# Linear attention and an MLP-Mixer block: the last 64 rows of all batches done as a ninth batch, and work moved from VectorE to ScalarE and GpSimd

## The chip, the cores and the metric

One core of a Trainium2 chip runs the whole program. The time is that of one execution on the device in microseconds; the median of several runs is given, and times are compared with those of the kernel before on the same chip. The engines have queues of their own and meet only through semaphores: TensorE (PE: matmul, with its weight loads, PEld), VectorE (DVE), ScalarE (ACT), GpSimd (POOL) and SyncE (SP, which here only issues transfers). The number behind an L is a line of the kernel before.

## What is computed

Eight batches, 8 heads, 576 positions, head dimension 64; the types are float32 at the outside.

```python
def _attn_ref(q, k, v):
    def phi(x):
        return np.where(x > 0, x, np.exp(x) - 1.0) + 1.0
    q_p, k_p = (phi(q), phi(k))
    kv = np.einsum('bhsd,bhse->bhde', k_p, v)
    z = np.sum(k_p, axis=2)
    num = np.einsum('bhsd,bhde->bhse', q_p, kv)
    den = np.einsum('bhsd,bhd->bhs', q_p, z)[..., None] + 1e-06
    return num / den

def _moe_ref(x, w_tok1, w_tok2, w_ch1, w_ch2):     # x: the heads side by side, 576 x 512 per batch
    xt = x.transpose(0, 2, 1)
    h = np.maximum(xt @ w_tok1, 0.0) @ w_tok2      # 576 -> 256 -> 576
    u = x + h.transpose(0, 2, 1)
    h2 = np.maximum(u @ w_ch1, 0.0) @ w_ch2        # 512 -> 1536 -> 512
    return u + h2
```

## The kernel before

**Tiling.** A batch's 576 positions are 64 partitions times 9; two of the nine share a tile of 128 rows, so a batch has four full tiles and a half one of 64 rows, its *tail*. Two batches' tails fill one tile: batches 2p and 2p+1 are pair p.

**An order written out by hand.** Every piece of work is a Python closure with a short name (`put`), and the string `ORDER` (L66) lists the names; each engine's queue holds its pieces in that order. No scheduler moves anything. `BANK` (L42) gives each result its PSUM bank, `SLOT` (L58) its place among the output slots of `obuf` (6 of 512 columns), `ON_DVE` (L36) the pieces that VectorE does where ScalarE would. A name begins with its batch: `3Lk0` loads half of k of batch 3 (on SP, float32, into one set of buffers that batches 0 and 2 to 7 share; batch 1 has its own), `3kx0` takes exp on ScalarE (L252), `3ka0` and `3kb0` finish phi on VectorE (L256, L262), `3v0` casts v (L275), `3K` is the kv product (L302), `3Kc0` its copy (L308), `3qT0` transposes q by a DMA on SP (L335).

**Numerators and denominators.** `3n` multiplies q by kv, 40 matmuls of 65 columns (64 numerators and their denominator) into three pairs of banks (L387). `3nd` and `3ne` take the reciprocals (L400, L402; L405, L407), then VectorE multiplies: three blocks of six heads-and-tiles, `3n0`, `3n1`, `3n2` (L413), and two single ones, `3o0`, `3o1` (L422). Batch 1 has a form of its own (`nd1_mm`, L352: 20 matmuls of 130 columns, in six groups with a reciprocal and a multiply each, L361 to L364).

**Token mixing.** `3f0`, `3f1` (L448), their relu on ScalarE (L452), `3g0`, `3g1` (L459), the add of x on VectorE (`3gu0`, L470), and the transposition of u by DMA (`3uT0`, L489). Batch 1 does the last steps by PE and copies (`1h`, L520 to L533; `1t`, `1tc`, L538 to L543). Tails: `3gt` makes those of a pair (L478), VectorE adds x into one of two tiles `ut` (L483), and a DMA transposes it (`3ut`, L494); pair 0 is transposed by PE (L672, L676).

**Channel mixing of the full tiles.** Batch 0, and batch 1's first layer, are plain matmuls (L686, L747). The rest treats each product as 2 x 2 blocks and takes it by seven block products, whose sums and differences of inputs are made beforehand. First layer: sums of u (`3s1` to `3s4`, VectorE, L885), of the weights once for all batches (`G`, into `swc`, L897), and for each of three groups seven products of four matmuls of 256 columns (`3x05` is product 5 of group 0, L928) with reads `3y05`: three copies and one relu by ScalarE (L943, L941), three add-and-relu by VectorE (L681). Batch 7 does not use `swc` but makes sums of its own (`7F`, GpSimd L869 and VectorE L836). Second layer: row sums of the activations (`3w`, L836), weight sums (`ws`, `wt`, once), seven products in two halves of six matmuls of 256 columns (`3p50`, L970). Three partial results are copied to SBUF by ScalarE (`3c0` to `3c2`, L1058); the four quarters of the output, Z, W, Y and X, are ended by VectorE, which adds u (`3eZ`, ..., L1064); GpSimd adds a copied part to Z, W and Y (`3hZ`, ..., L1071) and issues the stores (`3o`, L1075). Batches 1 to 6 use the same four output slots. Batch 7's ends are cut into 14 reads (`7R`, L984) and stores on SP and ScalarE's queue (`7D`, L990).

**Channel mixing of the tails.** Pairs 0 and 1, each in the middle of the order: `T00` to `T12` are 48 matmuls of 128 columns each pair (L711), read by ScalarE (L715), `U` 12 of 512 (L747), `V` the add of u (L760, output slots 4 and 5), `W` the stores by GpSimd. Pairs 2 and 3, at the end beside batch 7: `7c` is 48 matmuls of 256 columns (L733), read by ScalarE (L737), four sums by GpSimd (`7ts`, L836), seven products of six matmuls (`7t`, L1024), seven reads by VectorE (`7tr`, L1031), and stores of 128 KB.

Of the kernel before, what the change touches and what calls it, by code (L numbers as in the profile page):

```python
# [17 lines left out]
NO = 6  # L18
# [11 lines left out]
CUTS = {1: [0, 3, 6], 2: [0, 2, 6], 3: [0, 2, 6], 4: [0, 2, 6], 5: [0, 2, 6], 6: [0, 2, 6], 7: [0, 2, 4, 6]}  # L30
# [5 lines left out]
ON_DVE = {'1v0', '2v1', '0r3', '0r6', '0r9', '1r5', '1r8'}  # L36
# [3 lines left out]
WHOLE = {'00', '01', 't0', 't1'}  # L40

BANK = {k_: int(v_) for k_, v_ in (e.split(":") for e in """2K:0 2n0:0 2n1:2 2n2:4 2f:6 2g0:3 2g1:6 2X2:5 2Z2:2 2Y2:1 2gt:6 3K:6 3n0:2 3n1:4 3n2:6 3f:3 3g0:6 3g1:6 3X2:2  # L42
3Z2:0 3Y2:5 3gt:4 4K:2 4n0:2 4n1:4 4n2:6 4f:6 4g0:4 4g1:0 4X2:2 4Z2:1 4Y2:3 4gt:6 5K:6 5n0:1 5n1:3 5n2:5 5f:5
5g0:5 5g1:3 5X2:4 5Z2:5 5Y2:7 5gt:1 6K:2 6n0:1 6n1:3 6n2:5 6f:2 6g0:5 6g1:2 6X2:4 6Z2:0 6Y2:6 6gt:6 7K:2 7n0:2
7n1:4 7n2:6 7f:2 7g0:0 7g1:2 7X2:3 7Z2:6 7Y2:1 7gt:5 2m2:0 2m3:1 2m4:2 2m5:3 2m8:1 2m9:1 2m10:0 2m11:1 3m2:0
3m3:1 3m4:2 3m5:3 3m8:1 3m9:0 3m10:0 3m11:1 4m2:0 4m3:1 4m4:2 4m5:3 4m8:1 4m9:1 4m10:0 4m11:1 5m2:0 5m3:1
5m4:2 5m5:3 5m8:1 5m9:0 5m10:0 5m11:1 6m2:0 6m3:1 6m4:2 6m5:3 6m8:1 6m9:1 6m10:0 6m11:1 1h00:7 1h01:6 1h10:5
1h11:6 1t0:7 1t1:0 1t2:1 1t3:6 1m0:2 1m1:0 1m2:0 1m3:4 1m4:5 1m5:6 1m6:6 1m7:2 1m8:5 1m9:7 1m10:1 1m11:6 T00:7
T10:3 T01:3 T11:0 T02:3 T12:7 U08:0 U18:3 7c0:3 7c1:4 7c2:4 7c3:6 7c4:2 7c5:4 7X0:5 7Z0:4 7Y0:1 7X1:2 7Z1:0
7Y1:0 7PX0:7 7PZ0:3 7PY0:1 7PX1:6 7PZ1:5 7PY1:5 7tX:0 7tZ:4 7tY:2 1PX:1 1PZ:2 1PY:5 2PX:0 2PZ:5 2PY:1 3PX:0  # L50
3PZ:3 3PY:4 4PX:7 4PZ:0 4PY:0 5PX:0 5PZ:7 5PY:1 6PX:7 6PZ:1 6PY:6 warm0:0 0Q00:1 0Q01:2 0s0:3 warm1:0 0Q10:1
0Q11:2 warm2:3 0K0:4 0d0:0 0n0:6 0l0:1 0s1:2 0K1:4 0d1:3 0n1:6 0l1:0 0f0:1 0f1:4 0g00:2 0g01:3 0g10:0 0t0:6
0t1:4 0g11:1 0m0:3 0m1:7 0t2:6 0t3:4 0m2:1 0m3:2 0gt:2 0m4:5 0m5:6 0m6:6 0m7:3 0m8:7 0m9:0 0m10:4 0m11:4 U00:1
U01:0 1Q0:4 U02:2 U03:3 1Q1:6 1K:4 1n00:6 1n01:6 1n10:4 1n11:4 1n20:4 1n21:6 1f:4 1g2:4 0ut:3 2X1:6 2Z1:4
2Y1:2 3X1:3 3Z1:5 3Y1:1 4X1:7 4Z1:0 4Y1:0 5X1:6 5Z1:0 5Y1:2 6X1:5 6Z1:6 6Y1:1 2X0:7 2Z0:3 2Y0:0 3X0:4 3Z0:0
3Y0:6 4X0:1 4Z0:7 4Y0:5 5X0:1 5Z0:5 5Y0:0 6X0:7 6Z0:3 6Y0:2""".split())}

SLOT = {k_: int(v_) for k_, v_ in (e.split(":") for e in """0o0:0 0o1:2 1P:0 V0:4 2P:0 3P:0 V1:4 4P:0 5P:0 6P:0 7P0:4 7t:0 7P1:2""".split())}  # L58
# [7 lines left out]
ORDER = """A2 A0 A1 A3 A4 A5 A6 A8 A9 A7 A10 A12 A13 A14 A11 A16 A17 A15 A19 A18 A21 A20 A22 A23 A24 A25 A26 A27 A28 A29  # L66
A30 A33 A31 A32 A35 A34 A36 A37 A38 1Lk0 A39 1Lk1 1Lv1 A40 1Lq0 A41 1Lq1 A42 1Lv0 A43 0ma0 At2 0ma1 At3 0ma3
0mb1 0mb0 0ma6 0r0 0mb3 0r1 1ka0 0ma7 1kx0 0ma2 0ma8 0mb6 1kb0 0mb2 0r3 0mb8 0mb7 0r6 0r8 0ma4 0r7 G21 0gt
1kx1 G22 0ma9 0gv 0ma10 0mb4 1ka1 0r2 0ma5 0r4 G11 0mb10 1kb1 0mb5 0r10 G23 0mb9 0r5 0ma11 0mb11 1qa0 1qx0 B0
0r9 0q0 B1 0r11 1qb0 B2 1qx1 1qa1 1Q00 1Q01 0q1 1Qc01 1v0 1Qc00 0q2 1qb1 1v1 1Q10 1Q11 1K 1Qc11 2Lq0 ws02  # L70
1Qc10 0q3 2Lq1 1Kc0 1Kc1 2Lv0 ws04 1n20 1n01 2Lk0 1nc20 0q4 2Lk1 1nc01 2Lv1 1n10 0q5 1nc10 1n00 0q6 1nc00 1n11
0q7 1nc11 2qx0 1n21 ws14 0q8 1nc21 1f0 2qx1 2qa0 1f1 wt2 3Lq0 G24 0q9 1fr1 2qb0 1fr0 0q10 2qa1 2v0 G12 1h01
2qb1 1h00 1hu01 2qT1 ws00 0q11 1hu00 0z1 2kx0 1h10 2qT0 ws10 0z0 1h11 1hu10 1t0 1hu11 1t1 3Lv0 ws24 1g2 1tc1
1tc0 1t2 3Lq1 1t3 1gu2 1ma9 1tc3 ws12 0z2 1ma1 1ma5 1tc2 1ma4 0z3 1mb1 2v1 0o1 1mb5 1r1 1ma7 2ka0 2kx1 1mb7
G01 3Lk0 1ma10 0o0 G03 3qx0 1mb4 2kb0 0ut 1ma2 2ka1 1r4 1mb10 wt0 3Lk1 1mb2 1r7 1ma3 3Lv1 1r2 2kb1 1mb9 1r10
1ma8 3qa0 0uc 1mb8 1r5 ws20 1r9 2K 1r8 1mb3 2Kc0 2Kc1 3qb0 1ma6 1r3 2n ws30 2nd 1mb6 T00 2o0 ws34 1r6 2n1
1ma11 Tr00 2o1 ws22 1mb11 2ne 3v0 2n0 1ma0 1mb0 3qa1 T01 4Lv0 1r0 2n2 ws32 1r11 1p10 3qx1 2f0 1w13 G02 Tr01
# [38 lines left out]
def kernel(  # L116
# [1081 lines left out]
```

## Time and profile before

| | before |
|---|---|
| median of 3 runs (us) | 245.37 (245.18 to 245.67) |
| the profiled execution (us) | 245.24 |
| its span, first to last instruction (us) | 243.4 |
| granted TensorE clock | 0.998 |
| DVE busy between 72 and 80 us | 8.00 of 8.00 |
| ACT busy between 112 and 120 us | 7.16 of 8.00 |
| POOL busy between 112 and 120 us | 4.23 of 8.00 |
| loads of k, q and v (576 KB each), median from issue to landing (us) | 6.8, 6.3, 7.6 |
| stores by GpSimd, 512 KB, issue to landing (us) | 6.0 |
| DMA transposes of q, u and tails, issue to landing (us) | 4.7, 3.1, 2.5 |

"Busy" is the union of the instructions of an engine; matmuls overlap, so PE's busy time is not a measure of work done, and the spacing of matmuls must be read beside it. The line of an operation is that of the closure in which it stands. The groups of the costliest operations that the change touches (line, engine, operation, out <- in, shape, count | busy us, mean ns of one | idle before):

```profile
L711 PE MATMUL ps<-uTt,wc 128*128 128x128 bf16 x96 | 6.3, 219 | 0.1
L733 PE MATMUL ps<-uTt,wc 128*128 128x256 bf16 x48 | 5.9, 273 | 0.0
L413 DVE TENSOR_TENSOR x<-ps,dens 128x768 bf16<-128x768 f32 x18 | 16.6, 930 | 0.0
L619 ACT ACTIVATE x<-ps,den 128x64 bf16<-128x64 f32 x8 | 1.8, 324 | 0.0
```

### The profile page before, as it was taken

The numbers are of one execution on the slowest core, as the hardware profiler recorded it, in microseconds if no ns is written. First come the engines' busy times: TensorE is split into PE (matmuls) and PEld (weight loads), VectorE is DVE, ScalarE is ACT, GpSimd is POOL, SyncE is SP. The second block draws the span as 40 slices with busy tenths as digits, with TensorE's granted clock in tenths as the row PEclk, the third lists the DMA queues.
The fourth block names the chain that finished last, engine by engine and source line by source line (L and its number), as shares of the span: only waits on it lengthen the run. The fifth ranks groups of instructions, "written<-read, shape, count | busy, mean of one in ns | idle before, by whom it ended". The sixth has DMA issues, their size and how long they took to land.

```text
span 243.4 us, 6361 instructions
## 1 busy us (share of the span) xinstructions
PE 233.1 (96%) x2597; PEld 174.2 (72%) x2616; DVE 211.5 (87%) x387; ACT 136.4 (56%) x224; POOL 81.2 (33%) x88
## 2 busy tenths in 40 slices
PE   7889989999999999999999999999999999999991
PEld 3575445464677686789867887688778867888881
DVE  5955786999999989999999999999999599867661
ACT  4773782669788277327994297448923542347000
POOL 8870044076910620035200520206015810440730
PEclk9999999999999999999999999999999999999999
DMA  6999989999979989978948989495782285143035
GB/s 230 278 202 260 317 260 234 409 283 286 365 225 198 270 265 161 247 97 305 285 127 175 370 262 200 82 260 178 161 138 40 44 171 112 24 91 81 3 80 180
DMA packets 49805, 48.42 MB, mean 199 GB/s; under 512 B 30064, under 2 KB 35568, under 8 KB 49776
## 3 DMA queue, kind: packets, MB, share of 16 engines
q1 hardware_dynamic: 41664, 35.00, 51.3%
q0 software_dynamic: 7472, 12.22, 25.5%
q10 hardware_dynamic: 640, 0.79, 1.0%
q8 instruction: 20, 0.33, 0.6%
q14 instruction: 9, 0.07, 0.1%
HBM read 35.85 MB, written 9.44 MB: 186 GB/s over the span
## 4 chain that ended last, share of the span: by engine, by line
PE 84%; DMA 9%; POOL 3%; issue 1%; DVE 1%; SPq 1%; POOLq 0%; DVEq 0%
PE ps L970 27%; PE ps L928 23%; PE ps L747 6%; PE ps L448 6%; DMA q_raw<-in_q_dram 5%; PE ps L459 4%; PE ps L686 4%; DMA wc<-in_moe_w_ch_dram 4%; PE ps L711 2%; PE ps L733 2%; PE ps L302 2%; PE ps L1024 2%; PE ps L387 2%; POOL qT L1111 1%; POOL cr L233 1%
## 5 line engine op out<-in xcount | busy, mean ns | idle before, releaser
L970 PE MATMUL ps<-k_raw,v_raw 128*128 128x256 bf16 x252 | 31.8, 273 | 0.0
L943 ACT COPY v_raw<-ps 128x512 f32<-128x512 f32 x30 | 17.0, 595 | 22.7 <-PE ps L928 21.5
L970 PEld LDWEIGHTS <-cr 128*128 128x128 bf16 x252 | 24.4, 98 | 4.8
L970 PEld LDWEIGHTS <-v_raw 128*128 128x128 bf16 x252 | 24.1, 98 | 3.8 <-issue 0.4
L928 PEld LDWEIGHTS <-swc 128*128 128x128 bf16 x240 | 23.4, 98 | 3.1
L681 DVE CUSTOM_DVE_ANT_0 cr<-ps,v_raw 128x512 bf16<-128x512 f32 x30 | 20.1, 684 | 4.5 <-PE ps L928 2.5
L928 PEld LDWEIGHTS <-wc 128*128 128x128 bf16 x216 | 21.1, 98 | 3.6
L928 PE MATMUL ps<-crt,swc 128*128 128x256 bf16 x180 | 23.1, 273 | 0.0
L252 ACT ACTIVATE e<-q_raw 128x1152 bf16<-128x1152 f32 x16 | 18.7, 1167 | 6.7 <-DMA q_raw<-in_q_dram 6.7
L686 PE MATMUL ps<-uT,wc 128*128 128x512 bf16 x91 | 21.6, 379 | 0.4 <-issue 0.2
L970 PE MATMUL ps<-wc,cr 128*128 128x256 bf16 x168 | 21.6, 273 | 0.0
L1071 POOL TENSOR_TENSOR obuf<-obuf,w 128x512 f32<-128x512 f32 x6 | 8.2, 1360 | 38.6 <-ACT w L1058 19.5
L252 ACT ACTIVATE e<-k_raw 128x1152 bf16<-128x1152 f32 x16 | 18.5, 1166 | 3.2 <-DMA k_raw<-in_k_dram 2.6
L1071 POOL TENSOR_TENSOR obuf<-obuf,q_raw 128x512 f32<-128x512 f32 x6 | 8.2, 1374 | 35.6 <-DVE obuf L1064 35.6
L928 PE MATMUL ps<-uT,wc 128*128 128x256 bf16 x144 | 19.5, 273 | 0.0
L1064 DVE TENSOR_TENSOR obuf<-ps,u 128x512 f32<-128x512 f32 x24 | 16.4, 685 | 2.5 <-PE ps L970 2.4
L1071 POOL TENSOR_TENSOR obuf<-obuf,part 128x512 f32<-128x512 f32 x6 | 7.7, 1289 | 26.5 <-DVE dens L400 18.5
L413 DVE TENSOR_TENSOR x<-ps,dens 128x768 bf16<-128x768 f32 x18 | 16.6, 930 | 0.0
L686 PEld LDWEIGHTS <-wc 128*128 128x128 bf16 x96 | 8.9, 98 | 10.0 <-issue 0.6
L470 DVE TENSOR_TENSOR u<-ps,x 128x1024 bf16<-128x1024 f32 x12 | 14.6, 1220 | 0.1
L836 DVE TENSOR_TENSOR v_raw<-cr 128x512 bf16<-128x512 bf16 (+3 forms) x24 | 14.5, 620 | 0.0
L448 PE MATMUL ps<-x,w 128*128 128x512 bf16 x50 | 13.9, 379 | 0.3
(168 smaller groups left out, 514.3 us busy)
## 6 DMA issues: line engine op xcount, KB each, us to landing
k_raw<-in_k_dram SPq DMA_DIRECT2D x16, 576.0 KB, 6.8
q_raw<-in_q_dram SPq DMA_DIRECT2D x16, 576.0 KB, 6.3
v_raw<-in_v_dram SPq DMA_DIRECT2D x14, 576.0 KB, 7.6
out_dram<-obuf POOLq DMA_DIRECT2D x12, 512.0 KB, 6.0
wc<-in_moe_w_ch_dram POOLq DMA_DIRECT2D x8, 384.0 KB, 9.3
out_dram<-obuf POOLq DMA_DIRECT2D x4, 256.0 KB, 7.3
cr<-in_v_dram POOLq DMA_DIRECT2D x2, 288.0 KB, 7.6
out_dram<-obuf POOLq DMA_DIRECT2D x4, 128.0 KB, 4.8
```

The lines of the kernel that those rows point to most:

```text
L252: nc.scalar.activation(out=ebuf[EBUF[f"{n}{nm}{c}"]], in_=f, func=AF.Exp)
L413: nc.vector.tensor_tensor(out=xv[:, :, rc0:rc0 + 3], in0=nd_tile(n, m)[:, :, k0:k0 + 6, 0:D].rearrange("p i (q a) d -> p i q a d", a=2), i ...
L448: nc.tensor.matmul(out=banks(f"{n}f")[:, mt], lhsT=w1t[:, b, ms] if r == R else w1[:, r, ms], rhs=x[b][:, r, :], start=(r == 0), stop=(r = ...
L470: nc.vector.tensor_tensor(out=u[b][:, rs], in0=banks(f"{n}g{i}"), in1=x[b][:, rs], op=ALU.add)
L681: nc.vector._custom_dve(TENSOR_ADD_SAT, out=o, in0=ps, in1=c, s0=3.4028234663852886e38, s1=0.0)
L686: nc.tensor.matmul(out=bank(f"{n}m{mc}"), lhsT=wc1[:, kj, 128 * mc:128 * mc + 128], rhs=uTj[b][:, kj] if n < 2 - U1 else uT[b][:, :, kj], ...
L747: nc.tensor.matmul(out=bank(f"U{p}{t}"), lhsT=crt[:, kc, :] if t == 8 else cr[b][:, kc, 128 * r:128 * r + 128], rhs=wc2[:, kc, :], start=( ...
L928: nc.tensor.matmul(out=ps[:, j], lhsT=lhs[:, k_, 128 * j:128 * (j + 1)], rhs=rhs[:, :, k_], start=(first and j == 0 and k_ == 0), stop=(k_ ...
L943: nc.scalar.copy(out={1: c1, 6: c6, 5: c5}[i], in_=ps)
L970: nc.tensor.matmul(out=ps, lhsT=lhs[:, k_], rhs=rhs[:, k_], start=(first and not skip and k_ == 0), stop=(k_ == KH - 1), skip_group_check= ...
L1064: nc.vector.tensor_tensor(out=slots(f"{n}P", 4)[:, d::2, HC[c]], in0=pair_tile(n, "X" if z == "W" else z), in1=u[n % 2][:, d::2, HC[c]], o ...
L1071: nc.gpsimd.tensor_tensor(out=o, in0=o, in1=part[i], op=ALU.add)
```

## The change

**Tails.** `ut` and `uTt` get room for all four pairs (512 rows). The pieces `T`, `U`, `V`, `W`, `7c`, `7ts`, `7t`, `7tr` and `7td` go. In their place a ninth batch, named 8, passes through the closures of the block products: `8s`, `8x`, `8y`, `8w`, `8p`, `8c`, `8eZ` to `8eX`, `8hZ`, `8hW`, `8hY`, and four stores of 256 KB (`8o00` to `8o11`) on SP and ScalarE's queue. It has buffers of its own, cut from tiles that are no longer in use. Pair 0's transposition is a DMA now (`1ut`). Products of batches 7 and 8 alternate in the order. Batch 7 uses `swc`; the pieces `7F` go.

**Numerators.** Batch 1 takes the form of the others (`1na` and `1nb` are its two parts on PE, then `1nd`, `1n0` and so on). In batches 2 to 6 the third block, 12 heads-and-tiles, is done by ScalarE, one at a time, with the reciprocal as scale (`3n20`, `3n21`: six each).

**Ends.** In batches 1 to 5 the X and Y quarters are copied out of PSUM by ScalarE, and GpSimd adds u (`3lX`, `3lY`) as well as, for Y, the copied part.

**Small ones.** Two casts and reads of batches 1 and 2 go back to ScalarE (`2v1`, `1r5`, `1r8` leave `ON_DVE`), and two copies of batch 1 (`1tc0`, `1tc2`) go there. `obuf` has four slots. `ORDER` and `BANK` are written anew throughout.

```diff
-NO = 6
+NO = 4
-ON_DVE = {'1v0', '2v1', '0r3', '0r6', '0r9', '1r5', '1r8'}
+ON_DVE = {'1v0', '0r3', '0r6', '0r9'}
+ON_ACT = {'1tc0', '1tc2', '1eX', '1eY', '2eX', '2eY', '3eX', '3eY', '4eX', '4eY', '5eX', '5eY', '2n2', '3n2', '4n2', '5n2', '6n2'}
...
-    ut = [const(f"ut{i}", [128, DM]) for i in range(2)]
+    ut = const("ut", [128, 4, DM])
-    uTt = const("uTt", [128, 2, NDM, 128])
+    uTt = const("uTt", [128, 4, NDM, 128])
...
+    def nd_more(n, i):
+        xv = x[n % 2].rearrange("p r (c i a d) -> p i (r c) a d", c=2, i=2, a=2)
+        for k_ in range(6):
+            nc.scalar.activation(out=xv[:, i, 7 + k_ // 2, k_ % 2], in_=nd_tile(n, 2)[:, i, k_, 0:D],
+                                 func=AF.Copy, scale=last[:, i, k_:k_ + 1])
...
-    def ublock(h, e, b=1):
-        return uT[b][:, 2 * e:2 * e + 2, 2 * h:2 * h + 2]
+    def ublock(n, h, e):
+        if n < 2 - U1:
+            return uTj[n][:, 2 * h:2 * h + 2, 2 * e:2 * e + 2].transpose([0, 2, 1, 3])
+        return (uTt if n == B else uT[n % 2])[:, 2 * e:2 * e + 2, 2 * h:2 * h + 2]
...
     def mix_mm(n, g, i):
...
-        if n == B - 1:
-            s_, t, c0 = sw, tu, 256 * g
-        else:
-            s_, t, c0 = [swc[:, GSW[g], w] for w in range(4)], tuc, 0
+        s_ = [swc[:, GSW[g], w] for w in range(4)]
+        t = tu if n == B - 1 else tuc0 if n == 0 else tuc1 if n == 1 else tuc
...
-    for n in range(1, B):
+    for n in range(1, B + 1):
         for i in range(1, 8):
             for j in range(2):
                 put(f"{n}p{i}{j}", product, n, i, j)
...
     def pair_end(n, z):
         d, c = PAIR[z]
+        if f"{n}e{z}" in ON_ACT:
+            nc.scalar.copy(out=pair_out(n, z), in_=pair_tile(n, "X" if z == "W" else z))
+            return
...
+    def pair_u(n, z):
+        d, c = PAIR[z]
+        o = pair_out(n, z)
+        nc.gpsimd.tensor_tensor(out=o, in0=o, in1=(ut if n == B else u[n % 2])[:, d::2, HC[c]], op=ALU.add)
...
+    def tail_put(d, b):
+        (nc.sync, nc.scalar)[b].dma_start(
+            out=outv[2 * d + b::4, :, 2 * R].rearrange("n p d -> p n d"), in_=o8[d][half[b]])
```

Of the order, the stretch around batch 1's token mixing, and the last pieces (`1ma`, `1mb`: its first channel layer; `0q11`: the last block of batch 0's second layer; `0z`: its output adds):

```diff
-0q7 1nc11 2qx0 1n21 ws14 0q8 1nc21 1f0 2qx1 2qa0 1f1 wt2 3Lq0 G24 0q9 1fr1 2qb0 1fr0 0q10 2qa1 2v0 G12 1h01
-2qb1 1h00 1hu01 2qT1 ws00 0q11 1hu00 0z1 2kx0 1h10 2qT0 ws10 0z0 1h11 1hu10 1t0 1hu11 1t1 3Lv0 ws24 1g2 1tc1
+0q9 2kx0 2qa0 1f0 G12 3Lq0 2qb0 2qx1 1f1 2qa1 G03 0q10 3Lq1 1fr1 G21 2qb1 1fr0 0q11 2v0 0z0 2qT0 ws00 1h01 0z1
+1h00 2kx1 0z3 2qT1 ws10 1h10 1hu01 1hu00 1h11 0z2 1hu10 3Lv0 ws12 1t0 1t1 1hu11 1tc0 1g2 1t2 1tc1 2ka0 1t3
...
+8o10 8o11 7R51 7p50 7R61 7D210 7D211 7w42 7p20 7R50 8o00 7R60 7p71 7w44 7p31 7R71 7R20 7p30 7D710 7R31 7p70
+7D310 7D311 7R30 7p41 7D200 7D711 7R70 7p40 7D201 7R41 7D410 7D411 7R40 7D700 7D701"""
```

More of the change, by code (lines that the diff above doesn't have):

```diff
@@ L523, in mm2_half @@
                 nc.tensor.matmul(out=ps[:, i], lhsT=w2v(kt, r), rhs=ar[b][:, kt, cs],
-                                 start=(kt == 0 and k_ > 0), stop=(kt == NT - 1))
+                                 start=(kt == 0 and not (k_ == 0 and BY_PE)), stop=(kt == NT - 1))
     def mm2_half_read(c, k_):
@@ L765, in mm4_put @@
                                 in_=slots(f"0o{i}", 2)[half[e]])
-    def mm4_tail_put(p):
-        for b in range(2):
-            nc.gpsimd.dma_start(out=outv[2 * p + b, :, 2 * R], in_=slots(f"V{p}", 1)[half[b], 0])
     def m4_0(kc):
@@ L966, in product @@
             4: (a_(1, 1), tb[3], False), 3: (s_(3), wblock(1, 1), False)}[i]
-        skip = not first or (j == 1 and n < B - 1)
+        skip = not first or (j == 1 and n != B - 1)
         ps = product_tile(n, i, j)
@@ L991, in product_put @@
                                           in_=o[half[e], d, w])
-    for n in range(1, B):
+    for n in range(1, B + 1):
         for i in range(1, 8):
```

333 lines of the change are left out of this document (135 added, 198 removed).

## The prediction

> **What bounds the kernel now.** First the page: which engine is busy, and when.
>
> ```profile
> span 243.4 us, 6361 instructions
> PE 233.1 (96%) x2597; PEld 174.2 (72%) x2616; DVE 211.5 (87%) x387; ACT 136.4 (56%) x224; POOL 81.2 (33%) x88
> PE   7889989999999999999999999999999999999991
> DVE  5955786999999989999999999999999599867661
> ACT  4773782669788277327994297448923542347000
> ```
>
> PE is the candidate, but a busy share proves little: a 256-column matmul lasts 273 ns in the groups although the next one can start much sooner. The test is the spacing, so next the chain that ended last, in order of time (start, length, what):
>
> ```profile
> 33.13 0.61 DVE cr L693
> 33.78 0.81 PE ps L747 x3
> ...
> 39.18 0.42 PE ps L352 x6
> ...
> 46.96 1.73 PE ps L747 x8
> ...
> 112.14 0.89 PE ps L711 x16
> ...
> 158.16 0.72 PE ps L387 x40
> ...
> 216.44 0.87 PE ps L733 x8
> ...
> 234.56 1.31 PE ps L1024 x12
> ...
> 238.55 0.42 DVE obuf L1031
> ```
>
> Start to start: 1.31/12 = 0.109 us for 256 columns, 1.73/8 = 0.216 for 512, 0.89/16 = 0.0556 for 128, at every place of the chain from 33.8 to 238.5 us. All these are one column in 0.42 ns, and no piece between them is another engine's apart from scattered waits of 0.05 to 0.16 us. So PE runs its queue without a gap for 205 us: there a PE instruction removed is its spacing off the time, as long as the others keep pace. Before 33.8 the chain hangs on loads (the batch-1 q load from 18.8 to 31.9) and PE idles 0.84 us; after 238.5 there are 4.9 us of a last DVE add and the last stores.
>
> Can the others keep pace? Stretches (sums of busy us: PE, PEld, DVE, ACT, POOL, then clock, DMA share, GB/s):
>
> ```profile
> 60.00:66.00 6.00, 5.79 (x143) 3.63 (x144) 5.73 (x14) 4.29 (x9) 5.61 (x4) 1.00 1.02 389
> 102.00:108.00 6.00, 6.00 (x152) 4.97 (x151) 5.89 (x12) 2.43 (x5) 0.55 (x1) 1.00 0.96 120
> 60.62:104.37 43.75, 43.17 (x555) 32.34 (x566) 42.28 (x74) 28.63 (x44) 12.32 (x10) 1.00 0.98 246
> ```
>
> From the kv product of batch 2 (60.62) to that of batch 4 (104.37) DVE is busy 42.3 of 43.8 us: it is a second bound right behind PE. ACT and POOL have room.
>
> **The change on PE.** Removed: the tails of batches 0 to 3, 2 x 48 matmuls of 128 columns (L711) x 0.0556 = 5.34 and 2 x 12 of 512 (L747) x 0.216 = 5.18; the tails of batches 4 to 7, 48 of 256 (L733) and 42 of 256 (L1024) x 0.109 = 9.81; four transposes (L672), 0.22; batch 1's 20 numerator products (L352), whose five chain pieces add up to 1.30. Sum 21.85. Added: the ninth batch, 3 groups x 7 products x 4 = 84 and 7 x 2 x 6 = 84 matmuls of 256, 168 x 0.109 = 18.3; batch 1's numerators in the form of the others (40 of 65 columns, 0.72 at 158.16). Sum 19.0. Net -2.8 us. The columns alone say the same: 47,616 against 43,008 for the tails.
>
> **On DVE.** Its spacing when dense is its duration less about 0.08 (two of L681, 684 ns each, take 1.28 together: 0.60 each). Removed at such spacings: the X and Y ends of batches 1 to 5, 10 x 0.60; the third block of numerators of batches 2 to 6 (L413), 5 x 0.87; batch 7's weight sums (L836 on wc), 3 x 0.87; 7 tail reads (L1031) x 0.34; two tail adds (L760) 1.2; batch 1's numerators 5.2 in six triples against 3.7 in the new form; three reads or casts given to ACT, 1.9, and two copies, 0.7: 20.6 in all (1.5 net for batch 1). Added for the ninth batch: 9 add-relus x 0.60, 4 sums of u x 0.34, 6 row sums 3.6, 4 ends x 0.60: 12.8. Listing both orders item by item with these spacings gives -7.6 of 189.6 us, which I use (the measured 211.5 is by durations).
>
> **On ACT and POOL.** ACT takes 10 end copies x 0.48 (L1058, 587 ns long), and 60 pieces of numerators 128x64. The nearest row is L619, the same form in batch 0: eight in 1.75 us, 324 ns long each, so 0.20 apart if pipelined and 0.32 if not: 12.2 to 19.4; I take 0.20, since eight in a row were so. By my list ACT gains 20.9 in all. POOL takes 13 adds more (L1071, 1.26 free; 10 of them with a bf16 operand, for which the nearest rows are L816's, 1.16 to 1.79), 16 to 20 us, and loses the tail's four sums (6.8) and batch 7's six (4.2) and two store issues. All this lies beside PE if it fits. From one kv product to the next, by item and spacing (PE, DVE, ACT): batch 3 to 4 was 25.5, 24.7, 12.7 and becomes 24.2, 23.9, 19.2; batch 4 to 5 was 21.8, 21.6, 15.8 and becomes 23.7, 23.2, 20.8. (As a check, the old list gives 113.0 us of PE from the kv product of batch 2 to that of batch 7, whose chain pieces start 114.3 apart.) Over the whole order PE led DVE by 24 us and now leads by 29. So nothing outgrows PE on average; cost 0. If ACT's pieces did cost 0.32, batch 4 to 5 would be 22.2 of 23.7, still covered.
>
> **Moves and waits.** (1) Tails no longer fill gaps in the middle; that work stands at the end, where batches 7 and 8 alternate and fill for each other: PE 27.1 against DVE 21.0 and ACT 9.1 from the first product of batch 8 on. (2) The fourth tail transpose (issue 1.2 to 2.0, landing 2.4 to 3.4, so 3.6 to 5.4) is followed by the first sum of the ninth u on DVE 5.0 us of PE work later: up to 0.4 late, with batch 7's add-relus queued behind on DVE; DVE has 6 us of slack there: 0. SP has no loads left then. A transpose for pair 0 joins SP's queue between loads of batch 6, that much issue time: 0. (3) Ends now pass ACT, then POOL twice for Y; the single set of output slots is free later. From a batch's store issue to the next batch's first end there are 10.2 to 12.8 us of PE work (was 11.7 to 17.4); a 512 KB store lands in 6.0: covered. (4) Around batch 1's token mixing the new order has the last block of batch 0's product before the mixing products rather than among them. After it PE has 20 matmuls (2.2 us) and then the transposes, which need a DVE add queued behind three output adds: 4 x 0.60 = 2.4, started 0.5 before that point, so no wait if DVE is on time and 0.8 if it is one instruction late; the second pair of transposes meets the same. I take 0.4 (0 to 0.8). The load-bound start is the same in both orders, and PE's 0.84 there too: 0, or at best -0.84. (5) At the end four stores of 256 KB join; 128 KB from SP took 2.7 and 256 KB from POOL 7.3. On SP and ACT they stand ahead of most of batch 7's stores and wait for POOL's last adds (three, 1.3 each, from 10 us before the end). The last is issued 3.9 us of PE work before the end, so with 2.7 to 7.3 and 0.5 of issue it lands at most 3.9 after the last matmul, inside the present 4.9: 0, up to +1 if it crowds the last stores.
>
> Sum against the profiled execution (245.24, span 243.4): -2.8 + 0.4 = 242.8; the median of the runs shown is 0.13 above it: **243.0**.
>
> **Rivals.** *Ports.* In the trace GpSimd and DVE stretch each other: L885 takes 415 ns, but 621, 694 and 599 where a GpSimd tensor operation runs (187.6, 191.0, 210.7), and an L1071 add 1.26, at most 1.86. With five adds a batch instead of three, each meeting one or two such, DVE gets 0.2 to 0.28 x 5 = 1.0 to 1.4 longer per batch, where batches 3 to 5 have 0.3 to 0.5 to spare: PE would wait some 0.7 in two or three batches, 243.0 + 1.5 = 244.5. The Trainium skill (Trace Analysis, Optimizing Scalar/DVE Operations) warns of it: the two share an SBUF read port, so moving work between them might not help. By that rule the move to GpSimd gains nothing, which is this rival's time; the trace agrees that there are collisions, of 0.2 to 0.3 us each.
> *Loads, the slower side.* Without tails between them the kv products come earlier by PE's count: batch 3 by 5.3 us, batch 4 by 6.6, batch 6 by 15.4, with the same bytes to load. From batch 2's to batch 4's the DMA share was 0.98 over 43.75 us; the new order leaves 6.4 less (36.7 against 43.1 by the list), a share of 1.15. If about 1.0 is all the engines give, batch 4's inputs come up to 6 us late, in PE's queue nothing can pass, and half of that is 243.0 + 3 = 246.0, all of it 249; slower than before once they are 2.8 late. Against it: the stretches shown say that a share near 1 isn't a full pipe (389 GB/s at 1.02, 120 at 0.96, and 1.20 between 36 and 42); and the lead from issue to first use is 4.7 us of PE work at the shortest, then 6.6, against 5.2 and 5.4 before, with a median landing of 6.7.
> *Start.* The 0.84 at 33 us is filled and nothing is lost at (4): 245.37 - 2.8 - 0.8 = 241.8.
> *It doesn't do what it says:* PE's work falls but the bound is DVE with its waits; then its -7.6 is the gain or none of it, 238 to 245. The chain's even spacing excludes this for most of the span.
>
> **Chances.** Forecast (242.3 to 243.7) 0.50; start filled 0.09; ports 0.14, of which 0.01 within 0.2% of before; other small waits of 1 to 2 in sum, for instance for ACT's short pieces, 0.08 (0.01 within); DVE as the bound 0.02 (half and half); loads or another long wait 0.17, of which 0.02 within and 0.15 slower. Faster by over 0.2% (0.49 us, about what a measurement can tell from none): 0.50 + 0.09 + 0.13 + 0.07 + 0.01 = 0.80; same 0.01 + 0.01 + 0.01 + 0.02 = 0.05; slower 0.15. Range: 241.5 (all of PE's gain, the start filled and 0.25 for what the drain may give) to 246.0 (loads 3 late), leaving out about 0.05 below and 0.10 above; the likeliest alone 242.3 to 243.7.
>
> **What would show it.** PE's first-to-last matmul shorter by 2.4 to 2.8 us with the spacings unchanged; kv products of batches 3, 4 and 6 some 5, 6 and 15 us earlier; DVE busy about 8 less, ACT about 25 more by durations; no wait over 0.2 us in the chain after 55 us. Wrong if: pieces of POOL, ACT or a load stand in the chain after 55 us; PE idles between batch 2 and batch 5; L252 or L275 wait for a load; the 64-column pieces lie 0.3 apart and a token product waits for them; or the last store is one of the ninth batch's.

## The result, and the profile after

| | before | after |
|---|---|---|
| median (us) | 245.38 (245.18 to 245.67, 4 runs) | 248.47 (248.00 to 249.19, 4 runs) |
| ratio after/before, 95% interval | | 1.0128 (1.0099 to 1.0156) |
| the profiled execution, its span (us) | 245.24, 243.4 | 248.73, 246.9 |

The change makes the kernel 3.1 us slower; 243.0 was forecast. From here on a line number is that of the changed kernel: L705 is the plain first layer of batches 0 and 1, L728 batch 0's second, L892 and L934 the block products of the first and second layer, L476 and L487 token mixing, L424 the numerators on VectorE (L445 its single blocks) and L433 those on ScalarE, L411 to L418 the reciprocals, L264 and L270 phi's first and last step, L791 the weight sum `wt0`, L803 row sums, L845 sums of u, L783 GpSimd's weight sums, L742 batch 0's store issues, L985 the end copied by ScalarE, L987 an end on VectorE, L993 and L997 GpSimd's adds of u and of a part, L344, L517 and L522 the DMA transposes of q, u and tails, L334 the copy of batch 1's transposed q.

First the page's busy times and slices of the changed kernel:

```profile
span 246.9 us, 6402 instructions
PE 233.2 (94%) x2590; PEld 173.1 (70%) x2590; DVE 209.2 (85%) x369; ACT 157.8 (64%) x301; POOL 83.3 (34%) x87
...
PE   7889997999799999999999999899999999999992
...
DVE  5956593999999989999999999879895797969872
```

PE's row has three new dents, in slices 7, 11 and 26 (37 to 43, 62 to 68 and 154 to 160 us). DVE was to be 8 us less busy and is 2.3 less (209.2 against 211.5). ACT is 21.4 us busier, where some 25 were forecast by durations. PE's own list of waits after 36 us gives the dents a name (line, what was waited for, us in total, times, longest); before, this list had two entries of 0.2:

```profile
PE ps L934 <- DVE x L424: 1.9, 1, 1.9
PE ps L728 <- DMA wc<-in_moe_w_ch_dram: 1.5, 1, 1.5
PE ps L892 <- DMA uT<-u: 1.1, 1, 1.1
...
```

And the chain that ended last, in order of time, at these places and at a fourth (90 to 107 us):

```profile
32.55 5.94 DMA wc<-in_moe_w_ch_dram
...
38.54 1.02 PE ps L728 x4
...
64.56 1.90 DVE k_raw L791
...
67.28 0.96 DVE x L424
...
90.24 0.47 DVE cr L700
...
106.64 0.61 DVE obuf L987
...
138.69 0.50 ACT obuf L985
...
139.26 2.29 POOL obuf L993 x2
...
142.45 7.66 DMA out_dram<-obuf
...
153.82 4.54 DMA uT<-u
...
```

Before, this chain was PE's almost alone from 33.8 us to the end. Now it leaves PE for a weight load at 32.55, for VectorE at 64.56 and again from 90.24 to 107.24, and for ScalarE, GpSimd and a store from 138.69. The kv products of batches 3, 4 and 6 start at 76.84, 102.22 and 144.74: 1.7, 2.1 and 10.6 us earlier than before, where 5, 6 and 15 were forecast. If the 2.8 us of work are saved and the time is 3.1 longer, some 5.9 us of waits have come in.

The second place, by the timeline of VectorE and then of GpSimd (start, length, line, operation):

```profile
60.97 1.72 DVE L264 TENSOR_SCALAR y<-q_raw 128x1152 bf16<-128x1152 f32 x1
62.80 1.83 DVE L270 TENSOR_TENSOR qp<-e,y 128x1152 bf16<-128x1152 bf16 x1
64.55 1.91 DVE L791 TENSOR_TENSOR k_raw<-wc 128x1536 bf16<-128x1536 bf16 x1
...
```

```profile
60.27 2.54 POOL L742 DMA_DIRECT2D out_dram<-obuf  x4
62.83 4.64 POOL L783 TENSOR_TENSOR q_raw<-wc,q_raw 128x512 f32<-128x512 bf16 x3
```

Elsewhere L264 and L270 take 0.75 us and L791 took 0.95 before. While GpSimd issues four stores and then makes three sums, these three take 3.0 us more together, and the reciprocal behind them (66.7) is late. Over the whole span, VectorE's instructions that exceed the usual length of their form by over 0.1 us add up to 0.9 us before and 5.2 after. So 4.3 of the 5.7 us by which VectorE's busy time missed its forecast are such lengthenings.

### The profile page after: what moved, and what is told of

The parts are those of the page before. It is cut to its first block, busy times and chain, and to the rows that moved or that the text cites. A ratio compares the mean times of both kernels' runs of the same rounds, so it can differ in the third digit from the quotient of the medians.

```text
span 246.9 us, 6402 instructions
## 1 busy us (share of the span) xinstructions
PE 233.2 (94%) x2590; PEld 173.1 (70%) x2590; DVE 209.2 (85%) x369; ACT 157.8 (64%) x301; POOL 83.3 (34%) x87
## 4 chain that ended last, share of the span: by engine, by line
PE 65%; DMA 16%; DVE 9%; POOL 4%; issue 2%; ACT 1%; SPq 1%; POOLq 0%; DVEq 0%; ACTq 0%
PE ps L892 23%; PE ps L934 23%; DMA wc<-in_moe_w_ch_dram 6%; DMA q_raw<-in_q_dram 5%; PE ps L476 4%; PE ps L705 4%; PE ps L728 3%; DMA out_dram<-obuf 3%; PE ps L487 3%; DMA uT<-u 2%; PE ps L398 2%; PE ps L310 1%; DVE cr L700 1%; DVE u L498 1%; POOL obuf L993 1%
## 5 line engine op out<-in xcount | busy, mean ns | idle before, releaser
L892 PEld LDWEIGHTS <-swc 128*128 128x128 bf16 x336 | 32.9, 98 | 4.5
L934 PEld LDWEIGHTS <-cr 128*128 128x128 bf16 x288 | 28.0, 98 | 7.8 <-issue 2.8
L934 PE MATMUL ps<-k_raw,v_raw 128*128 128x256 bf16 x252 | 31.8, 273 | 0.0
L892 PE MATMUL ps<-crt,swc 128*128 128x256 bf16 x216 | 28.3, 273 | 0.0
L934 PEld LDWEIGHTS <-v_raw 128*128 128x128 bf16 x252 | 23.9, 98 | 5.4 <-DVE v_raw L803 1.3
L892 PEld LDWEIGHTS <-wc 128*128 128x128 bf16 x252 | 24.6, 98 | 4.4 <-DMA uT<-u 1.4
L934 PE MATMUL ps<-wc,cr 128*128 128x256 bf16 x192 | 24.1, 273 | 1.9 <-DVE x L424 1.9
L997 POOL TENSOR_TENSOR obuf<-obuf,q_raw 128x512 f32<-128x512 f32 x6 | 8.7, 1454 | 43.8 <-DVE obuf L987 33.3
L705 PE MATMUL ps<-uT,wc 128*128 128x512 bf16 x96 | 22.3, 379 | 0.4 <-ACT cr L714 0.4
L997 POOL TENSOR_TENSOR obuf<-obuf,part 128x512 f32<-128x512 f32 x6 | 7.7, 1288 | 36.6 <-DVE dens L411 28.5
L892 PE MATMUL ps<-uT,wc 128*128 128x256 bf16 x144 | 18.7, 273 | 1.1 <-DMA uT<-u 1.1
L705 PEld LDWEIGHTS <-wc 128*128 128x128 bf16 x96 | 9.0, 98 | 11.1 <-issue 1.5
L433 ACT ACTIVATE x<-ps,dens 128x64 bf16<-128x64 f32 x60 | 13.0, 342 | 5.1 <-DVE dens L418 4.9
L803 DVE TENSOR_TENSOR v_raw<-cr 128x512 bf16<-128x512 bf16 (+3 forms) x24 | 14.6, 617 | 1.2 <-ACT cr L905 1.2
L264 DVE TENSOR_SCALAR y<-k_raw 128x1152 bf16<-128x1152 f32 x16 | 12.0, 753 | 3.7 <-DMA k_raw<-in_k_dram 3.6
L424 DVE TENSOR_TENSOR x<-ps,dens 128x768 bf16<-128x768 f32 x16 | 15.0, 947 | 0.1
L283 ACT CAST vs<-v_raw 128x1152 bf16<-128x1152 f32 x13 | 14.8, 1171 | 0.0
```

The source lines that it names most:

```text
L283: copy(out=vs[:, js, :, 0:D], in_=raw["v", rb(n)][:, js].rearrange("p j (t d) -> p j t d", t=T))
L424: nc.vector.tensor_tensor(out=xv[:, :, rc0:rc0 + 3], in0=nd_tile(n, m)[:, :, k0:k0 + 6, 0:D].rearrange("p i (q a) d -> p i q a d", a=2), i ...
L433: nc.scalar.activation(out=xv[:, i, 7 + k_ // 2, k_ % 2], in_=nd_tile(n, 2)[:, i, k_, 0:D], func=AF.Copy, scale=last[:, i, k_:k_ + 1])
L705: nc.tensor.matmul(out=bank(f"{n}m{mc}"), lhsT=wc1[:, kj, 128 * mc:128 * mc + 128], rhs=uTj[b][:, kj] if n < 2 - U1 else uT[b][:, :, kj], ...
L803: return engine.tensor_tensor(out=s_[which - 1][:, ks], in0=x_, in1=y_, op=op)
L892: nc.tensor.matmul(out=ps[:, j], lhsT=lhs[:, k_, 128 * j:128 * (j + 1)], rhs=rhs[:, :, k_], start=(first and j == 0 and k_ == 0), stop=(k_ ...
```

## Experiments

The first theory was "four waits": the weight load at the start, VectorE locked out at 61 to 66 us, VectorE at its limit from 90 to 107, and an output store that comes late at 150. Ratios are to the kernel before (245.3 to 245.7 in each set of runs), with their 95% interval.

**One edit for each of three waits, then all three.**

```diff
 e1_start: the order
-1Qc11 0q3 2Lq0 ws02 1Qc10 2Lk0 1K 2Lq1
+1Qc11 2Lq0 ws02 1Qc10 2Lk0 1K 0q3 2Lq1
 e2_sums: ws22 waits for batch 2's first reciprocal, ws34 and ws32 follow it
-(2, 0): ("phi", "k", 2, 1)}
+(2, 0): ("phi", "k", 2, 1), (2, 2): ("den", 2)}
 e3_ends3: '3eX' and '3eY' leave ON_ACT, 3lX and 3lY leave the order
```

> The changed kernel, with the fourth block of batch 0's second layer (0q3) behind the kv product of batch 1 instead of ahead of it. After the change PE stands 1.53 us at 37.0 for a transfer of weights that lands at 38.5. Theory 'four waits' (the PE saving of 2.8 us is real and is given back in four places: this wait, DVE held up by GpSimd between 61 and 66 us, DVE at its limit between 90 and 107, output slots that come free late at 150 to 158): the kv product can start when its last cast ends (about 37.5), takes 0.7, so the wait shrinks to about 0.4 + 0.4: 0.7 us faster than the changed kernel, 247.8 (247.4 to 248.2). Rival 'one queue' (DVE is the bound up to 107 us and what is won before goes into its queue): no gain, 248.2 to 248.7, the kv product of batch 4 where it was (102.2).

Measured: 247.78, ratio 1.0101 (1.0084 to 1.0119), 0.7 below the changed kernel's ratio, as "four waits" said. The 1.5 us wait became one of 1.0 for a copy of q.

> The changed kernel, with GpSimd's weight sums ws22, ws34 and ws32 held back until batch 2's first reciprocal, so that no GpSimd sum runs while VectorE does qp and wt0 at 62.8 to 66.5 us; same work. 'Four waits': these two take 0.75 and 0.95 instead of 1.83 and 1.91, the reciprocal comes about 2.0 us earlier, PE's wait of 1.90 at 66.4 goes, 246.6 (246.3 to 247.2); y at 61.0 stays long (1.7), since the four store issues beside it stay. 'One queue': the kv product of batch 3 comes 1.9 earlier but that of batch 4 at most 0.7, 247.8 or more. If the long durations have another cause than GpSimd's sums, they stay and so does the time.

Measured: 247.05, 1.0051 (1.0034 to 1.0069): 1.9 us won by the ratios (1.4 by the medians; nine of the twelve runs lie between 246.6 and 247.5, three between 245.4 and 245.8), and PE's wait of 1.9 is gone. The same stretch of VectorE in this kernel:

```profile
60.72 0.76 DVE L264 TENSOR_SCALAR y<-q_raw 128x1152 bf16<-128x1152 f32 x1
...
62.27 0.95 DVE L791 TENSOR_TENSOR k_raw<-wc 128x1536 bf16<-128x1536 bf16 x1
...
67.07 1.51 DVE L803 TENSOR_TENSOR v_raw<-cr 128x768 bf16<-128x768 bf16 x1
```

Usual lengths again, and VectorE now waits 0.85 for PE at 63.2. L264 is short too, against the expectation, although the store issues still stand beside it (60.02 to 62.79): this time GpSimd was the one that waited, its second issue took 0.94 where it took 0.61 in the changed kernel. The last line is a new meeting: one of the sums, moved, now locks out a row sum (0.55 us elsewhere).

> The changed kernel, with the X and Y ends of batch 3 alone back on VectorE in one instruction each (GpSimd's two adds of u go). 'Four waits': the store of batch 3 is issued some 2.3 us earlier than at 141.8, the first end of batch 4 doesn't wait for it at 150, PE's idle 1.1 at 158.4 goes: 247.3 (246.9 to 247.8). Rival 'the transposes of u are late by themselves, or VectorE misses the 1.2 us': 248.2 to 249.2, PE still idle near 158.

Measured: 247.02, 1.0064 (1.0040 to 1.0087), 1.6 us won by the ratios, and PE's wait at 158 is gone. In the profiled executions the stretch between the kv products of batches 6 and 7 is 1.1 shorter (25.3 against 26.4); another 0.65 lies between those of batches 3 and 4, ahead of all that the edit touches.

> The three edits of the other runs together. 'Four waits': the gains add, 0.7 + 1.9 + 1.2 = 3.8, 244.7 (244.2 to 245.4), faster than the kernel before. 'One queue': 246.5 or more, with VectorE dense from 61 to 107 us and the gain of the third edit alone left. 'The ninth batch costs more than it saves' (its PE saving is not real): the waits go but the time stays over 247.

Measured: 245.43, 1.0005 (0.9984 to 1.0027): 3.0 of the 3.8 us by the ratios, and 0.7 above the 244.7 expected. The waits are those of single places and nearly add, but what is left is only even with the kernel before.

**Which wait was it at 158?** The third edit brought what was expected of it, for a wrong reason, though the chain names the store. VectorE doesn't stand still anywhere between 140 and 152 us of the changed kernel, so it never waited for an output slot; and with the edit its first end of batch 4 starts at 151.62 instead of 152.03, no real difference. SP's queue differs. The changed kernel, then the run with batch 3's ends on VectorE:

```profile
145.60 5.46 SPq L344 DMA_TRANSPOSE qT<-qp  x2
151.11 1.26 SPq L522 DMA_TRANSPOSE uTt<-ut  x1
152.47 2.61 SPq L517 DMA_TRANSPOSE uT<-u  x2
```

```profile
145.19 3.37 SPq L344 DMA_TRANSPOSE qT<-qp  x2
148.61 1.59 SPq L522 DMA_TRANSPOSE uTt<-ut  x1
150.31 2.67 SPq L517 DMA_TRANSPOSE uT<-u  x2
```

In the changed kernel the store is issued at 141.83 and lands at 150.12; the two transposes of q are held on SP beside it for 5.5 us. With the store issued at 139.76 it is 3.4. (The profiled kernels with a ninth batch all fit this: where the store is issued 3.8 us ahead of them they hold SP for 4.7 to 5.5, four kernels; where it is 5.4 to 5.7 ahead, for 2.9 to 4.3, eleven kernels. No run moves the store alone, so that the store is the cause of the holding is not shown.) Behind them stands the transpose of a tail, and only then that of u, whose data were ready at about 149.4. To see whether the queue is the cause, the tail's transpose alone was moved:

```diff
 e15_tail, and e16_clear_tail on the version below
-5gu1 3ut 4p60 4p61 7ka1 5uT1 ... 4eZ 5uT0
+5gu1 4p60 4p61 7ka1 5uT1 ... 4eZ 5uT0 3ut
```

> The changed kernel, with one thing moved: the DMA transpose of pair 1's tail (3ut) stands behind the two transposes of batch 5's u on SP, not ahead of them. 'SP's queue': the first transpose of u is issued 1.3 us earlier than at 152.5, lands earlier by as much, PE's wait of 1.1 at 158.4 goes: 1.0 to 1.2 faster, 247.4. 'Output slots that come free late', as expected before: no change, 248.2 to 248.7, with PE still waiting near 158.

Measured: 247.35, 1.0072 (1.0050 to 1.0094): 1.1 us (1.4 by the ratios) by a move on SP that changes no other engine's order. The first transpose of u is issued at 151.16, and PE's list of waits has the other two entries alone. SP's queue it was, not the output slots.

> The same move in the version with the sums laid clear and batch 3's ends on VectorE (244.5), where PE doesn't wait at that place any more. 'SP's queue': no change within 0.3. Only if something else hangs on that queue, 0.3 to 0.6 faster.

Measured: 244.70, 0.9966 (0.9945 to 0.9987), against 244.48 and 0.9940 without the move: no gain, where nothing waits.

**What VectorE and GpSimd do to each other**, measured by itself:

> Five kinds of VectorE instruction, six of each: alone, beside 48 GpSimd float32 adds of 128x512, and beside 28 GpSimd store issues; nothing of the computation, the outputs hold constants. Alone as in the kernels: 0.75 (phi's float32 step), 0.75 (bfloat16 minimum of two), 0.41 (sum of u), 0.69 (an end from PSUM), 0.68 (relu from PSUM). 'One locks the other': the first three are lengthened beside GpSimd's adds, by up to the whole of an add (1.16) when the add was first, and GpSimd's adds are lengthened when VectorE was first; those that read PSUM stay as they are. Beside the issues the same, by up to an issue (0.6). Rival 'a shared bandwidth': all are longer by the same few tenths.

The timeline of VectorE, alone (first three lines), then beside GpSimd's adds (last three), six instructions a line, total length each:

```profile
14.46 4.71 DVE L58 TENSOR_TENSOR f<-e,y 128x1152 bf16<-128x1152 bf16 x6
19.09 2.72 DVE L59 TENSOR_TENSOR ud<-ua,ub 128x512 bf16<-128x512 bf16 x6
21.72 4.31 DVE L60 TENSOR_TENSOR od<-ps,ua 128x512 f32<-128x512 f32 x6
...
39.85 10.48 DVE L58 TENSOR_TENSOR f<-e,y 128x1152 bf16<-128x1152 bf16 x6
50.26 8.48 DVE L59 TENSOR_TENSOR ud<-ua,ub 128x512 bf16<-128x512 bf16 x6
58.66 4.30 DVE L60 TENSOR_TENSOR od<-ps,ua 128x512 f32<-128x512 f32 x6
```

"One locks the other" holds: the kinds that read only SBUF get (10.48 - 4.71)/6 = 0.96 us longer each, (8.48 - 2.72)/6 = 0.96 as well, whatever their own length; those that read PSUM stay as they are. So the two engines do not meet through semaphores alone. The float32 step goes from 4.72 to 9.43 for its six (one of which ran before the adds began). GpSimd's adds take 1.66 beside the first two kinds, 1.32 beside the third and 1.26 alone. So it is no shared bandwidth but turns, one instruction each. The Trainium skill (SBUF — State Buffer, Who interferes with whom) says that the shared port pair of the two is an exclusive lock, and that a VectorE instruction with two SBUF inputs contends with a GpSimd instruction that reads SBUF; the trace agrees, with 0.96 us for L58 and L59.

The 0.96 is no constant of the hardware: it is what the add had left. In the steady stream VectorE's instruction begins when the add beside it has 1.09 us to go, and takes 0.95 longer. In the kernel before, the three L885 that the prediction shows begin when GpSimd's instruction has 0.34, 0.41 and 0.31 left, and take 0.21, 0.28 and 0.18 longer; in the changed kernel L270 at 62.80 has 1.20 left before it and takes 1.08 longer, L791 at 64.55 has 1.10 and takes 0.96. In all meetings with a GpSimd tensor operation in the profiled kernels that lengthen VectorE's instruction by over 0.15 us, it gets longer by what GpSimd's has left, less 0.12 to 0.14.

Beside the store issues only one of thirty was longer, by 0.17, and the issues themselves took up to 0.80 instead of 0.59; the 0.97 that L264 lost to them in the changed kernel isn't seen here.

**Is the moved work worth moving?** Two parts of the change undone in the kernel of the three edits:

```diff
 e6_n2dve: '2n2' to '6n2' leave ON_ACT; Nn20 Nn21 -> Nn2 in the order
 e7_endsdve: '1eX' '1eY' '2eX' '2eY' '4eX' '4eY' '5eX' '5eY' leave it; no lX, lY
```

> The kernel of the three edits, with the third block of numerators of batches 2 to 6 back on VectorE (5 x 0.87 us there, 60 short pieces less on ScalarE). If VectorE is the second bound between 61 and 107 us, the blocks of batches 2, 3 and 4 are paid at least in half: 1.5 slower than the three edits, 246.9 (246.2 to 248.0). Rival 'the short pieces are what hurts, they keep ScalarE from PE's reads': 0.3 to 1 faster, under 245.1.

Measured: 249.30, 1.0154 (1.0132 to 1.0177), 3.7 us slower than the three edits by the ratios for 4.4 us of VectorE work: far more than expected. PE's waits there (after 36 us) are VectorE's without exception:

```profile
...
PE ps L892 <- DVE x L445: 1.0, 1, 1.0
PE ps L934 <- DVE obuf L987: 0.8, 1, 0.8
...
```

Not all of this is the work put back: another of these waits, 0.6, is for a sum of u (L845) that a GpSimd add locks out at 83.74; it takes 1.07 longer.

> The kernel of the three edits, with the X and Y ends of batches 1, 2, 4 and 5 too on VectorE (8 x 0.60 us there; ScalarE loses 8 copies, GpSimd 8 adds of 1.1 to 1.9). If VectorE's time decides, the ends of batches 1 and 2, which lie between 80 and 107 us, cost about half of their 2.4: 1.0 slower, 246.4 (245.8 to 247.2). Rival 'GpSimd's adds cost as much by meeting VectorE as they save': no change or up to 0.8 faster.

Measured: 247.86, 1.0103 (1.0081 to 1.0125), 2.4 slower for 4.8 us, more than expected too. So both moves help in this order, the ends in spite of GpSimd's adds (the ends of batch 4 alone make no difference, below); the new order has no room on VectorE.

**Room on VectorE between 61 and 72 us.**

```diff
 e5_wt0: the three edits, and
-2K 0o0 1r1 3Lv1 wt0 1ma3
+ws04 wt0 2Lv0    (at 38.5 us)
 e9_room: e5_wt0, 3ka0 ahead of 2nd, ws32 behind 1w23 and waiting for it
 e10_room4: e9_room, and '4eX' '4eY' leave ON_ACT
 e11_clear: e5_wt0, but ws22 not held back; ws34 waits for the reciprocal
 e12_load: e11_clear, 4Lq0 ahead of 2uT1, its gate removed
```

> The kernel of the three edits, with the weight sum wt0 (0.95 us on VectorE, before batch 2's first reciprocal at 63.5 us) moved to 38.5 us, where VectorE stands idle for 3.3 us and its weights have landed. 'Four waits', now with the part that is left: VectorE is the chain from 63.5 to 71.6 and PE waits 0.53 there for a row sum, so 0.5 faster than the three edits' 245.4: 244.9 (244.5 to 245.3). Rival: it only meets GpSimd elsewhere, no change.

Measured: 245.40, 1.0003 (0.9981 to 1.0024): no change; the rival held.

> The three edits, and in the stretch from 61 to 72 us, where VectorE still sets the end: wt0 at 38.5 us, the first step of phi for batch 3 (3ka0, 0.67) ahead of batch 2's first reciprocal, where VectorE waits 0.9 for PE, and the last weight sum ws32 held back on GpSimd until batch 1's last row sum, so that it can't lock VectorE out of a row sum (1.52 instead of 0.55 at 66.5 in the three edits). VectorE's chain from 63.5 to 71.6 gets 1.6 shorter and PE's wait of 0.53 at 71 goes with its late products: 0.7 faster than the three edits, 244.7 (244.2 to 245.2). If the meetings of the two engines only move on, as with wt0 alone: 245.4.

Measured: 245.49, 1.0008 (0.9985 to 1.0030): no change. (Here and in the next, ws32 reads a buffer that a copied part has overwritten by then, so one weight sum has other values; the instructions are the same.) The kv product of batch 3 came 0.5 earlier and that of batch 4 0.5 later than in the three edits; in between VectorE waited 1.2 us for the load of batch 4's q.

> The kernel before this one, with the X and Y ends of batch 4 on VectorE too (2 x 0.60 there, two GpSimd adds less). If VectorE's time decides: 0.3 to 0.8 slower than the one without. If it is again the store that comes late and GpSimd's adds that lock, as with batch 3: 0.5 to 1.2 faster, 243.5 to 244.3.

Measured: 245.50, 1.0010 (0.9989 to 1.0030): neither theory; batch 4's ends make no difference.

> The three edits with wt0 at 38.5 us, and GpSimd's sums laid where VectorE reads PSUM or stands idle: ws22 behind the store issues at 62.2 (VectorE idle there), ws34 and ws32 beside batch 2's numerators at 64 to 66.4. No row sum is locked out (1.52 us at 66.5 in the three edits), VectorE's chain from 63.5 to 71.6 is 0.97 shorter, PE's wait of 0.53 at 71 goes: 244.9. If VectorE then only waits at 88 us for the load of batch 4's q, as the run with the shifted phi step showed (1.2 us), the gain is lost there and it stays at 245.4.

Measured: 244.48, 0.9940 (0.9925 to 0.9955): 1.5 us faster than the kernel before by the ratio, from seven runs. Two versions that differ from it only in one moved transfer that takes no wait from PE, e12_load and e16_clear_tail, lie at 0.9953 and 0.9966, so the gain is 0.8 to 1.5. No row sum from 68 to 72 us is lengthened, and PE's list has no wait over 0.2 after 39 us. Expected over the three edits were 0.5, measured 1.0 by the medians and 1.6 by the ratios. In the profiled executions the stretch aimed at, between the kv products of batches 2 and 3, is the expected 0.5 shorter (12.86 against 13.40); where the surplus comes from wasn't found.

> The same, and the load of batch 4's first q half (4Lq0) sent before the transposes of batch 2's u instead of behind them and behind two other loads, without its gate. VectorE no longer waits for it at 88 us (0.9 in the changed kernel, 1.2 with the shifted phi step): the kv product of batch 4 comes 0.5 to 1.0 earlier than without, 244.2 (243.7 to 244.8), faster than the kernel before by 1 us. Rival: the load takes bandwidth from the transposes of u, which land later, PE waits there instead: 245.2 or more.

Measured: 244.72, 0.9953 (0.9933 to 0.9974). VectorE's wait for the load is gone and the time is the same: nothing hung on it.

**Is PE's saving there at all?**

```diff
 e13_light on e11_clear, e14_before_light on the kernel before
+m = 2 * TD if n == 0 else TD
-nc.vector.tensor_scalar(out=ybuf[YBUF[f"{n}{nm}{c}"]], in0=f, scalar1=1.0, scalar2=1.0,
+nc.vector.tensor_scalar(out=ybuf[YBUF[f"{n}{nm}{c}"]][:, 0:m], in0=f[:, 0:m], scalar1=1.0, scalar2=1.0,
```

> The version with the sums laid clear (244.5), with the first step of phi (0.75 us) done on half its columns in batches 1 to 7: 28 x 0.3 = 8.4 us less on VectorE, that half of the step left out, PE's, ScalarE's and GpSimd's work the same. 'VectorE holds back the rest of PE's saving': PE's remaining small waits go, 1.0 to 1.5 faster, 243.0 to 243.5. 'PE alone is the bound by now and the ninth batch costs more than counted': 244.3 to 244.6.

Measured: 244.13, 0.9949 (0.9922 to 0.9976): by the interval no different from 244.48.

> The kernel before, lightened in the same way (8.4 us less on VectorE, half of the step left out). If it was bound by PE with VectorE covered, as the prediction took it: within 0.3 of 245.4, and 2.4 to 2.8 above the other lightened kernel, which is PE's saving. If VectorE held it too: 0.5 to 1.5 faster.

Measured: 245.41, 0.9995 (0.9980 to 1.0010): 8.4 us less on VectorE change nothing, the kernel before was PE's. Between the two lightened kernels lie 1.3 us. In their profiled executions the time from the kv product of batch 2 to the last matmul is 176.1 against 178.1 (178.0 in the kernel before, 176.6 in e11_clear, 180.1 in the changed kernel).

## Why the prediction was wrong

- *PE bounds the kernel; a PE instruction removed is its spacing off the time "as long as the others keep pace".* The first half is shown by the lightened kernel before. The saving of 2.8 is not seen whole, and the forecast's own items say why. Of these only the tails and the ninth batch lie behind the kv product of batch 2, 20.33 - 18.3 = 2.0; two matmuls of 512 columns more (L705, batch 1's first layer) were put ahead of it, 12 behind it instead of 14, which makes 2.4. Measured there, with the large waits gone, are 2.0 (176.1 against 178.1); the 0.4 between are waits of under 0.3 us each. The other 0.8 (batch 1's numerators and the four transposes, 1.30 + 0.22 - 0.72) lie ahead of that product. With them, less the two matmuls, it should have come 0.4 earlier than before; it starts at 60.6 in the kernel before (61.1 lightened) and at 60.9 to 62.6 in the kernels with the first edit. So the saving ahead of batch 2 is lost, and more. PE waits 1.0 there for the copy of q (L334), which the kernel before doesn't; how much of the rest is the scatter of the first loads stays open.
- *"So nothing outgrows PE on average; cost 0."* This step failed. The averages were about right (24.6 and 23.9 us from kv product 3 to 4 and 4 to 5 in the lightened kernel, against 24.2 and 23.7), with 0.3 to 0.5 us a batch to spare, but a margin that thin is no cover: two instructions that GpSimd's sums locked out were enough to stop PE for 1.9 us. Putting 4.4 us of VectorE's work back cost 3.7, putting 4.8 back another way 2.4, taking 8.4 away gained nothing sure. VectorE stands just at PE's edge: more costs half or nearly all of itself, less gains nothing.
- *The ports rival* had the mechanism and the wrong price: 0.2 to 0.28 for a meeting, from three rows of the trace before in which GpSimd's instruction was nearly over, 0.31 to 0.41 us from its end. Met near its start it costs 0.96 to 1.08. With 1.9 us in one place this alone is most of the gain that was forecast. Of the Trainium skill's warning that the prediction weighed (Perfetto Trace Analysis, Optimizing Scalar/DVE Operations: work moved between VectorE and GpSimd might not help) the trace bears out the collisions, but not that the move was worth nothing: with the ends of four batches back on VectorE the kernel was 2.4 us slower. (The numerators, 3.7, went to ScalarE.)
- *"The load-bound start is the same in both orders ...: 0, or at best -0.84."* The load nearly was (those weights land at 37.7 and at 38.5); the order was not. The block that needs them had stood behind the kv product and was put ahead of it: 0.7 by the first edit.
- *"A transpose for pair 0 joins SP's queue between loads of batch 6, that much issue time: 0"* and *"covered"* for the output slots. The slots were covered. The queue was not: the prediction counted the one new transpose, of pair 0, and missed that pair 1's had been put just ahead of batch 5's u, behind two transposes of q that take 5.5 us where the store of batch 3 comes late: 1.1 to 1.6.
- *Loads late, the slower side,* got the sign, and with up to 249 even the size, by luck: apart from the weights at the start no load stopped PE, and removing VectorE's wait for one gained nothing.
- Sizes that held: 60 short pieces on ScalarE, 2.57 us for twelve, 0.21 apart (0.20 taken); GpSimd's adds of u 1.15 to 1.55 (1.16 to 1.79); tails at the end, no cost (from the kv product of batch 7 to the last matmul PE has no wait that its list shows).
- *The fourth place of the first theory*, VectorE at its limit from 90 to 107 us, was never a large one: PE waited 0.4 there by its list, from kv product 3 to 4 it took 25.4 against 24.6 with the three edits, and the one edit aimed at it (that of the last load) gained nothing.

In sum: two moves and one undone pair of ends took back the 3.1 us that were lost (3.0 by the ratios), and GpSimd's sums laid beside PSUM work, with `wt0` moved, brought 0.8 to 1.5 of the 2.4 forecast.

## What to carry to other kernels

When the bounding engine gets less work, ask at each place what the second engine has to spare, in single instructions and not on average, and what one lost turn would do there. Work for GpSimd belongs beside VectorE work that reads PSUM, or beside its idle time. A transfer that is moved is moved in its queue: list what stands behind it there, and which of that PE waits for.

## What was not expected of the hardware

- A meeting with a GpSimd tensor operation costs VectorE not a share of its own instruction but what GpSimd's has left, less 0.12 to 0.14 us: 0.18 with 0.31 left, 0.96 with 1.10, 1.08 with 1.20.
- Who goes first can hang on an instruction that comes later. Beside the same four store issues, and begun 0.70 us after the first of them in every profiled kernel, phi's first step took 1.72 in the seven kernels in which the sum `ws22` follows the issues at once (the changed kernel among them) and 0.76 in the seven in which `ws22` is held back; halved in columns, with `ws22` at once, 1.43. Each of these is a profiled execution of another kernel and none falls out, so chance is unlikely; why the later sum matters stays open.
- The executions of a kernel scatter unequally: the three edits' twelve runs lie from 244.6 to 247.5, the kernel before's beside them, 23 runs, from 244.4 to 246.2. The cause wasn't tested.
- Two transposes of q held SP's queue for 4.7 to 5.5 us where a store had been issued 3.8 us ahead of them, and for 2.9 to 4.3 where it was 5.4 to 5.7 ahead.
